# A fourth weight group taken from rounded parts, and a hand-kept list of steps made anew

## The chip, the cores and the metric

The kernel runs on one core of one Trainium2 chip. The metric is the device time of one execution in microseconds (us). An execution's time is a little longer than the span that its profile shows from the first to the last instruction; both are given below.

## What is computed

The reference has two stages. The first is a gated linear attention over 4 batches, 8 heads, 768 tokens and a head width of 48; the second is a feed-forward block on the 3072 resulting rows of width 384, with 2048 hidden columns.

```python
f = 1.0 / (1.0 + np.exp(-f_logit))
for t in range(S):
    state = f[:, :, t, :, None] * state + einsum('bhd,bhde', k[:, :, t], v[:, :, t])   # outer product
    y[:, :, t] = einsum('bhd,bhde->bhe', q[:, :, t], state)
x = y as rows (B*S, H*D)                    # 3072 x 384
h = x @ w_in                                # first product, 384 -> 2048
sp = np.maximum(h, 0.0) + np.log1p(np.exp(-np.abs(h)))
g = h * erf(sp)
out = g @ w_out                             # second product, 2048 -> 384
```

## The kernel before

**Tiling.** The tokens are cut into 24 chunks of 128 rows (numbered g), two of which make one of 12 blocks of 256 rows (blk). For a block the 2048 hidden columns are four groups of 512 (gi = 0 to 3). For every group the first product leaves a 128x1024 tile `h`; ScalarE (ACT) takes an exponential and three hyperbolic tangents, VectorE (DVE) three combining passes, and the second product multiplies the result by the rows of `w_out` that belong to the group, adding up all four groups of a block in one bank pair of PSUM. `copy_rows` and `store` then send the block's 256 output rows away. The weights come in as 64-bit numbers and are rounded at the start (the steps named `r`, on ACT and DVE).

**Plain products and products from parts.** A float32 product is done in one of two ways. *Plain*, one float32 matmul, which is two recorded instructions on TensorE (PE). *From parts*: the activation is cut into a (ACT, `part_a`), b and t (DVE, `part_b` and `part_t`), the weight into three streams, and three matmuls of the type fp32r, one recorded instruction each, are added up in PSUM. The first three blocks take the first product plain, the later nine from parts. The second product is plain in blocks 0 to 3; from block 4 on it comes from parts for the groups in `SPLIT_OUT`, which are 0, 1 and 2, and stays plain for group 3. Of a weight of the second product, one part (`form_o`) stays in SBUF in the place of the plain weight; the two others are written to `form_dram` once (`keep_form`) and fetched again by every block in pieces of 384 KB (`fetch_form`, on the POOL queue; 2 streams x 2 pieces a group).

**Buffers.** 15 slots of 128x1024 words (`slot(n, ...)`) hold the tiles e, x, h, g, the fetched pieces, kT, qA, lt and rows by turns; a slot's new owner waits until the last reader of the old one is done. PSUM is four bank pairs. Two copies of v with the running state (`sv`) and two states are used in turn; from chunk 12 on the state goes into `sv` by DMA from the SP queue (`copy_state` without an engine, L554 before), in earlier chunks by a copy on ACT or DVE.

**What sets the order.** One long list, `STEPS`, gives the program order: each token is a step (name, numbers, engine letter, and after @ the slots or bank pairs). Every engine and every DMA queue takes its own instructions strictly in the order of the list and waits for semaphores. The names used below: `d` sums of logits, `tx` transposes, `ds` state products (L571), `sc` scores (L583), `y` the attention's output rows (L634), `st` adding up the state (L547 and L548, DVE), `sp` state into `sv`, `hf`/`ht` the first product from parts (L695), `ae` exponential (L173), `ax`/`aw` the two tanh terms (L176), `at`/`au` the passes that take them in (L181), `ah` the last tanh (L726), `am` the last multiply (L730), `ka`/`kb`/`kt` the parts of the activation (L737, L741, L750), `nc`/`no` fetches (L391), `oa`/`o`/`ot` the second product (L762; `oa` with part a, `o` with b or plain, `ot` with t), `cl`/`ex`/`ln` the logits, `z` dummy matmuls (L433) that occupy PE at the start. ACT loads a table whenever it changes between `ex`/`ln` and the tanh steps.

Of the kernel before, what the change touches and what calls it, by code (L numbers as in the profile page):

```python
# [81 lines left out]
def kernel(  # L82
# [347 lines left out]
    def keep_busy(n):  # L430

        for _ in range(n):
            nc.tensor.matmul(busy[-1], lhsT=tri[:], rhs=tri[:], start=True, stop=True)  # L433
# [389 lines left out]
    def pads(_):  # L823
# [6 lines left out]
        p0 f0@0 f1 k0 zb0@0 in0 v1 r0_0 q0 cl0 r0_1 ex0 v0 r0_2 ln0 cl1 q1 r0_3 z21 d0@1 ex1 ln1  # L830
        k1 r0_4 e0 z2 d1@2 r0_5 p2 to0@1 e1 qd0 f2@0 r0_6 tq0@3 v0_0_0a p1 v0_1_1a to1@2 ta0 kd0
        aq0@1 q2 qd1 tk0 ta1 kd1 v0_0_1a ds0 ak0v@2 ds1 v0_1_0a st0 sc0 ms0 sp0a st1 tq1@3 q3
        v1_1_0a m0_1_1 v1_0_0a tk1 f3 aq1@2 st2 ak1v@3 v1_1_1a cl2 z4 sc1 v1_0_1a m0_0_0 sp1a
        m0_1_0 m0_0_1 v3 ex2 m1_1_1 r1_0 v2 m1_0_0 z7 y0_1@1 m1_0_1 ln2 k2 r1_1 y0_0 sp2a st3
        d2@3 x0a p3 m1_1_0 r2_0 y1_0@1 cl3 r1_2 k3 y1_1 e2 r2_1 w3 r1_3 p6 x1a to2@3 v2_1_1a
        v2_1_0a r2_2 p7 h0_0@1 v2_0_0a r1_4 v2_0_1a f4@2 ta2 ex3 r1_5 ln3 r2_3 sp3a r1_6 d3@0 p5
        r2_4 r3_0 h0_1 p4 qd2 r2_5 e3 r3_1 kd2 f5 tq2@0 kd3 r6_0 r2_6 tk2 aq2@0 ds2 r3_2 ds3@2
        ak2v@1 to3 qd3 c0_0a v4 r6_1 sc2 v5 r3_3 ae0_0@3 h0_2@1 m2_0_0 ax0_0@1 r3_4 m2_0_1 r3_5
        tq3@0 st4 aw0_0@4 tk3 r3_6 q5 aq3@5 m2_1_0 h0_3 k4 st5 k5 r4_0 ak3v@6 m2_1_1 sp4a r4_1
        f7@7 r5_0 ta3 sc3 r4_2 st6 y2_1@3 c0_1a y2_0 m3_0_1 sp6a m3_1_1 w4 m3_1_0 sp5a f6 m3_0_0  # L840
        y3_1@1 x2a st7 y3_0 ae0_1@0 r5_1 cl4 x3a sp7a r5_2 h1_0@1 w5 r4_3 ex4 q4 r5_3 r4_4 r7_0
        r5_4 h1_3@2 r4_5 ln4 r7_1 r5_5 r4_6 d4@3 d5@0 e4 h1_1 r5_6 p8 f8@2 kd4 r6_2 e5 qd4 r6_3
        tx4@0 c1_0a@5 r7_2 to4@3 p9 qd5 aq4@6 f9 r6_4 h1_2 ak4v@8 r6_5 r8_0 r7_3 q7 sc4 r6_6
        c1_1a@9 k6 ds4 r7_4 h0_5@0 m4_1_0 v6 r7_5 r9_0 p10 m4_0_0 r7_6 q6 h0_4 m4_0_1 p11 m4_1_1
        ta4 kd5 at0_0 k7 tx5@2 c0_2a st8 to5@1 ak5v@1 sp8a st9 ds5 aq5@8 au0_0 h0_7@3 aw0_1@10
        v7 ta5 r9_1 r8_1 r9_2 st10 sc5 sp9a r9_3 h0_6 sp10a m5_0_1 r10_0 r9_4 r11_0 m5_1_1
        m5_1_0 ax0_1@1 r10_1 y4_1@2 m5_0_0 y4_0 r10_2 c0_3a y5_0@1 w6 at0_1 y5_1 ah0_0 h1_4@3
        r10_3 ax0_2@1 am0_0 x5a x4a w7 au0_1 ae0_2@3 h1_5 r9_5 ax0_3@10 r11_1 ah0_1 r9_6 h2_2@2
        c1_2a@8 at0_2 p13 kco1@6@4 am0_1 aw0_2@1 sCo1 h1_7@3 r11_2 ae1_0@0 r10_4 r11_3 r10_5
        h2_3 r11_4 au0_2 nc4_1@11 r10_6 ah0_2 h1_6 r11_5 p14 c2_1a@1 am0_2 ax1_0@12 r11_6  # L850
        ae0_3@3 h2_0@2 at1_0 p15 c1_3a@13 at0_3 aw1_0@12 h2_4@3 r8_2 aw0_3@10 au1_0 r14_0 au0_3
        ah1_0 h2_1 r8_3 ah0_3 am1_0 r15_0 r8_4 ax1_1@10 h2_5 r15_1 r8_5 c2_0a@0 am0_3 aw1_1@12
        h2_6@2 r15_2 r13_0 r8_6 ae1_3@3 r13_1 p12 r15_3 ae1_1@14 o1_0_0@1 r13_2 at1_1 r13_3
        ax1_2@10 o0_0_1@0 r14_1 r13_4 r15_4 au1_1 r12_0 o1_0_1 r14_2 aw1_2@12 r12_1 r13_5 r12_2
        kMo1 o0_0_0 c2_2a@5 r12_3 sMo1 r13_6 ah1_1 r12_4 o0_1_0 r15_5 am1_1 kci0 kci1 r12_5
        o0_1_1 ae1_2@14 r15_6 r12_6 at1_2 o0_2_1 kci2 r14_3 ax1_3@10 au1_2 kci3 o0_2_0 at1_3
        ah1_2 aw1_3@12 r14_4 am1_2 aw2_0@10 o1_1_0 au1_3 ae2_0@14 r14_5 kci4 cl6 ah1_3 o1_1_1
        r14_6 ex6 kMi2 kMi0 o0_3_1 am1_3 ax2_0@9 cl8 kMi1 o0_3_0 kMi4 ae2_1@3 at2_0 ln6 kMi3
        o1_2_0 au2_0 ro0a@9 ax2_1@12 kDi2 ms6 d6@0 kDi0 so0 d7@3 h2_7 e6 at2_1 f11@7 ah2_0 qd6
        e7 kd6 kDi3 aw2_1@12 tx6@3 td7 am2_0 o1_3_0 q8 c2_3a@9 k8 ak6v@10 aq6@14 td6 kd7 qd7 f10  # L860
        kci6 au2_1 sc6@3 kci5 ds6 m6_0_1 tx7@2 kci7 m6_1_1 o1_2_1 kMi5 v8 aq7@10 ak7v@12 tt6
        ah2_1 m6_1_0 k9 kDi4 q9 ex8 o1_3_1 am2_1 tt7 kDi5 ax2_2@3 m6_0_0 ds7@2 st12 cl10 y6_0@0
        v9 st13 sc7 kDi1 o2_0_1@3 sp12a sp13a m7_0_1 st14 ro1a@12 m7_1_0 ae2_2@13 so1 m7_1_1
        m7_0_0 y6_1 sp14a at2_2 y7_0@1 aw2_2@8 w8 y7_1 o2_1_1 kMi6 xa6 xa7 st15 ex10 xb7 w9 xb6
        xt7 hf3_2@0 xt6 aw2_3@12 au2_2 ht3_2 hf3_0@1 ah2_2 kMi7 hf3_1 ln10 kDi6 am2_2 ht3_1
# [379 lines left out]
```

## Time and profile before

| | us |
|---|---|
| median of 3 runs (585.39 to 588.98) | 588.85 |
| the profiled execution's own time | 588.31 |
| its span, first to last instruction | 586.3 |
| PE busy | 559.7 |
| DVE busy | 465.5 |
| ACT busy | 428.9 |
| POOL busy | 106.2 |

Busy times are unions of an engine's instructions; PE's instructions are pipelined, so that its rate is read from the distance of starts and not from the durations. DMA moved 85.59 MB. All rows used further on come from this one execution.

### The profile page before, as it was taken

The page shows a single profiled execution, that of the slowest core. Times are in us where ns is not written, and L with a number is a line of the kernel's source. Part 1 is how long each engine was busy: PE and PEld are TensorE (multiplying, and loading weights), DVE is VectorE, ACT ScalarE, POOL GpSimd, SP SyncE. Part 2 cuts the span into 40 slices and gives each one's busy share as a digit, 9 for nine tenths or more (in the row PEclk, how much of TensorE's full clock was granted, in tenths as well). Part 3 has the DMA queues.
Part 4 walks back from the last instruction along what each step waited for, and adds up shares of the span by engine and source line. Part 5 has one row for each costly group of instructions (what it writes and reads, how often), then busy time and mean ns, then how long its engine had stood idle before and what let it go on. Part 6 is the DMA issues. An engine that isn't in the chain of part 4 may idle for free.

```text
span 586.3 us, 14905 instructions
## 1 busy us (share of the span) xinstructions
PE 559.7 (95%) x6189; PEld 470.5 (80%) x6189; DVE 465.5 (79%) x657; ACT 428.9 (73%) x529; POOL 106.2 (18%) x191
## 2 busy tenths in 40 slices
PE   8888999999999999999979999999998999999995
PEld 7776888855678668888859888979888979897983
DVE  6888999999995697886589889498966886686491
ACT  5768497859999875984998995678782853682781
POOL 1103021000030003033032123142233114211020
PEclk9979999999999999999989999999998999999999
DMA  8996755200540286199339669545888176565071
GB/s 212 227 262 124 188 152 183 100 27 0 115 107 1 42 232 213 55 234 224 81 86 213 177 150 220 125 128 162 218 225 188 38 182 168 166 184 155 28 200 47
DMA packets 155698, 85.59 MB, mean 146 GB/s; under 512 B 132228, under 2 KB 135300, under 8 KB 155624
## 3 DMA queue, kind: packets, MB, share of 16 engines
q1 hardware_dynamic: 139112, 42.68, 31.7%
q0 software_dynamic: 16512, 41.89, 25.5%
q8 instruction: 51, 0.84, 0.6%
q14 instruction: 23, 0.19, 0.1%
HBM read 73.41 MB, written 9.51 MB: 141 GB/s over the span
## 4 chain that ended last, share of the span: by engine, by line
PE 66%; ACT 10%; DVE 9%; DMA 7%; issue 3%; SPq 3%; POOL 0%; ACTq 0%; DVEq 0%; POOLq 0%
PE pair L762 27%; PE pair L695 21%; PE pair L676 8%; PE pair L634 3%; DVE e L181 2%; PE pair L583 2%; DMA raw_y<-in_moe_w_in_dram 2%; ACT qA L519 2%; DMA sv<-state 2%; ACT x L176 2%; PE pair L571 1%; PE pair L433 1%; DMA piece<-form_dram 1%; DVE qA L608 1%; DMA lt<-in_f_logit_dram 1%
## 5 line engine op out<-in xcount | busy, mean ns | idle before, releaser
L181 DVE SCALAR_TENSOR_TENSOR e<-x,e 128x1024 f32<-128x1024 f32 x96 | 116.6, 1219 | 36.9 <-ACT e L173 19.3
L176 ACT ACTIVATE x<-h,serf_bias 128x1024 f32<-128x1024 f32 x88 | 100.0, 1147 | 15.9 <-DVE e L181 11.0
L762 PE MATMUL pair<-plain_o,h 128*128 128x384 f32 x320 | 110.5, 493 | 0.8 <-DVE h L730 0.8
L391 POOL DMA_DIRECT2D piece<-form_dram x96 | 52.2, 545 | 282.6 <-PE pair L762 169.0
L762 PEld LDWEIGHTS pair<-plain_o,h 128*128 128x128 f32 x320 | 59.0, 191 | 37.9 <-DVE h L730 1.1
L288 POOL DMA_DIRECT2D sv<-in_v_dram x84 | 52.4, 635 | 180.2 <-PE pair L634 156.8
L762 PE MATMUL pair<-piece,g 128*128 128x384 f32 x384 | 81.6, 350 | 1.7 <-DMA piece<-form_dram 0.8
L695 PE MATMUL pair<-xT,form_x 128*128 128x256 f32 x432 | 77.0, 286 | 0.4 <-DVE xT L657 0.4
L695 PE MATMUL pair<-xT,form_i 128*128 128x256 f32 x432 | 74.1, 279 | 0.0
L762 PEld LDWEIGHTS pair<-piece,g 128*128 128x128 f32 x384 | 66.5, 191 | 5.8 <-DVE g L750 1.1
L676 PE MATMUL pair<-xT,plain_i 128*128 128x256 f32 x288 | 67.8, 394 | 1.2 <-ACT xT L137 0.8
L726 ACT ACTIVATE e<-e 128x1024 f32<-128x1024 f32 x48 | 50.5, 1055 | 21.3 <-DVE e L181 20.9
L695 PEld LDWEIGHTS pair<-xT,form_x 128*128 128x128 f32 x432 | 62.5, 188 | 4.5 <-DVE xT L657 1.4
L676 PEld LDWEIGHTS pair<-xT,plain_i 128*128 128x128 f32 x288 | 55.4, 196 | 10.4 <-ACT xT L137 1.0
L695 PE MATMUL pair<-xT,form_y 128*128 128x256 f32 x432 | 62.4, 283 | 0.0
L730 DVE TENSOR_TENSOR h<-h,e 128x1024 f32<-128x1024 f32 x44 | 53.5, 1219 | 9.5 <-ACT e L726 9.5
L695 PEld LDWEIGHTS pair<-xT,form_i 128*128 128x128 f32 x432 | 60.9, 188 | 0.0
L695 PEld LDWEIGHTS pair<-xT,form_y 128*128 128x128 f32 x432 | 56.4, 188 | 1.6 <-issue 0.3
L173 ACT ACTIVATE e<-h 128x1024 f32<-128x1024 f32 x44 | 46.1, 1051 | 12.9 <-DVE h L137 7.1
L137 ACT COPY h<-pair 128x1024 f32<-128x1024 f32 x34 | 34.2, 1009 | 21.6 <-PE pair L695 10.3
L608 DVE TENSOR_TENSOR qA<-pair,tri 64x256 f32<-64x256 f32 x96 | 40.4, 421 | 7.0 <-PE pair L571 3.3
L762 PE MATMUL pair<-form_o,g 128*128 128x384 f32 x192 | 39.8, 340 | 0.0
(104 smaller groups left out, 777.4 us busy)
## 6 DMA issues: line engine op xcount, KB each, us to landing
piece<-form_dram POOLq DMA_DIRECT2D x96, 384.0 KB, 3.9
raw_y<-in_moe_w_out_dram SPq DMA_DIRECT2D x8, 768.0 KB
kn<-in_k_dram SPq DMA_DIRECT2D x24, 192.0 KB
vt<-in_v_dram SPq DMA_DIRECT2D x24, 192.0 KB
qn<-in_q_dram SPq DMA_DIRECT2D x24, 192.0 KB
form_dram<-piece SPq DMA_DIRECT2D x12, 384.0 KB
out_dram<-rows SPq DMA_DIRECT2D x12, 384.0 KB
sv<-in_v_dram POOLq DMA_DIRECT2D x84, 48.0 KB, 3.0
```

Source lines behind the costliest of these rows:

```text
L137: (engine.copy if engine is nc.scalar else engine.tensor_copy)(out=out, in_=in_)
L173: nc.scalar.activation(out=dst[:], in_=h, func=AF.Exp)
L176: nc.scalar.activation(out=dst[:], in_=h, func=AF.Tanh, bias=serf_bias[:, i : i + 1], scale=SERF_KAB[i][0])
L181: nc.vector.scalar_tensor_tensor(out=e[:], in0=x[:], scalar=SERF_KAB[i][2], in1=e[:], op0=ALU.add, op1=ALU.mult)
L288: nc.gpsimd.dma_start(out=svs[g % NSV][half(1 - r), r, c, :, PAD : PAD + D], in_=v[b, r::2, t0 : t0 + C, :].rearrange("a t d -> t a d"),)
L391: nc.gpsimd.dma_start(out=streams[i, blk, u], in_=form_dram[i, u])
L608: nc.vector.tensor_tensor(out=to, in0=sc[half(c), r], in1=tri1[half(c)].unsqueeze(1).broadcast_to((C, HP, C)), op=ALU.mult,)
L676: nc.tensor.matmul(hts[blk, gi][:, 2 * i + j, :], lhsT=w[:, kt, j * P : (j + 1) * P], rhs=xTs[blk][:, 0, kt, :], start=(kt == 0), stop=(kt ...
L695: nc.tensor.matmul(hts[blk, gi][:, 2 * i + j, :], lhsT=w[:, kt, j * P : (j + 1) * P], rhs=x[:, kt, :], start=(blk, p) not in begun, stop=True,
L726: nc.scalar.activation(out=e[:], in_=e[:], func=AF.Tanh, scale=SERF_C)
L730: nc.vector.tensor_tensor(out=h, in0=h, in1=es.pop((blk, gi))[:], op=ALU.mult)
L762: nc.tensor.matmul(ots[blk][:, tt, 0:d_model], lhsT=lhs, rhs=rhs, start=("o", blk, tt) not in begun, stop=True, skip_group_check=True,)
```

## The change

`SPLIT_OUT` becomes (0, 1, 2, 3): from block 4 on group 3 of the second product comes from parts as well. So 8 x 1 `ka`, `kb` and `kt`, 32 fetches (`nc`, `no` with u = 6 and 7) and 64 plain products become 192 products from parts; and once, at the making of the parts, 2 more `kco`, `kMo` and `kDo` and 4 stores of 384 KB. `keep_busy` can put its dummy matmuls into a bank pair that a later step will own, and there are 43 dummy products instead of 34. The list of steps is new throughout, 1962 tokens instead of 1862, from a planning run in which the transfer times were those of the packets in a trace. The number of ACT table loads is 32 in both.

```diff
+    ahead = {}
+
     def bank_pair(n):
-        return psum.tile([P, 2, 512], FP32, name=f"pair{n}", tag=f"pair{n}")
+        return ahead.pop(n, None) or psum.tile([P, 2, 512], FP32, name=f"pair{n}", tag=f"pair{n}")
...
-    SPLIT_OUT = (0, 1, 2)
+    SPLIT_OUT = (0, 1, 2, 3)
...
-    def keep_busy(n):
-
-        for _ in range(n):
-            nc.tensor.matmul(busy[-1], lhsT=tri[:], rhs=tri[:], start=True, stop=True)
+    def keep_busy(times, n=None):
+        to = busy[-1]
+        if n is not None:
+            ahead[n] = bank_pair(n)
+            to = ahead[n][:, 0, 0:P]
+        for _ in range(times):
+            nc.tensor.matmul(to, lhsT=tri[:], rhs=tri[:], start=True, stop=True)
...
     STEPS = """
...
-        no11_5@3 kb11_2 oa11_4 oa11_5 au11_3 o11_2_0_1 kt11_2 ah11_3 o11_2_1_1 am11_3 ot11_4
-        ot11_5 o11_3_0 o11_3_1 ro11a@1 so11
...
+        nc11_6@12 oa11_5 au11_3 o11_2_1_1 nc11_7@0 o11_2_0_1 ah11_3 ot11_4 am11_3 no11_6@7
+        ot11_5 ka11_3@10@9 no11_7@1 kb11_3 oa11_6 oa11_7 kt11_3 o11_3_1_1 o11_3_0_1 ot11_6
+        ot11_7 ro11a@1 so11
     """.split()
```

Three places of the new order. First, PE at the end of the program, block 11, the last block; a row is a run of instructions, with the bank pair written and what is read: `xT` and `form_x`, `form_i`, `form_y` are the first product, `g` the parts of the activation, `piece` and `form_o` weights from parts, `plain_o` the plain weight. Before:

```order
L762 MATMUL pair_6436<-piece,g 128x384 x4
L695 MATMUL pair_6362<-xT_6269,form_y_1704 128x256 x6
L762 MATMUL pair_6436<-piece,g 128x384 x8
L816 MATMUL pair_6511<-ident,low 1x128
L762 MATMUL pair_6436<-piece,g 128x384 x4
L762 MATMUL pair_6436<-form_o_2295,g 128x384 x8
L762 MATMUL pair_6436<-piece,g 128x384 x16
L762 MATMUL pair_6436<-form_o_2354,g 128x384 x8
L762 MATMUL pair_6436<-piece,g 128x384 x8
L762 MATMUL pair_6436<-plain_o_1180,h 128x384 x8
```

The same place now:

```order
L767 MATMUL pair_6666<-piece,g 128x384 x8
L700 MATMUL pair_6558<-xT_6431,form_y_1707 128x256 x6
L767 MATMUL pair_6666<-form_o_2335,g 128x384 x8
L767 MATMUL pair_6666<-piece,g 128x384 x16
L767 MATMUL pair_6666<-form_o_2492,g 128x384 x8
L767 MATMUL pair_6666<-piece,g 128x384 x16
L767 MATMUL pair_6666<-form_o_2920,g 128x384 x8
L767 MATMUL pair_6666<-piece,g 128x384 x8
```

After the last run of the first product, 52 products from parts and 8 plain ones have become 64 from parts.

Second, ACT at the start of the third batch of sequences, where the logits of two blocks are taken (L422 and L426 before, L424 and L428 now) between the tanh terms of blocks 4 and 5; `qA` is the copy that frees a bank pair of transposes for PE. Before:

```order
L402 ACT_TABLE_LOAD
L426 ACTIVATE lt<-lt 128x768
L176 ACT_TABLE_LOAD
L176 ACTIVATE x<-h,serf_bias 128x1024
L402 ACT_TABLE_LOAD
L422 ACTIVATE lt<-lt 128x768
L176 ACT_TABLE_LOAD
L176 ACTIVATE x<-h,serf_bias 128x1024
L173 ACTIVATE e<-h 128x1024
L402 ACT_TABLE_LOAD
L426 ACTIVATE lt<-lt 128x768
L519 COPY qA<-pair_3109 64x512 x2
```

Now:

```order
L137 COPY h<-pair_2863 128x1024
L424 ACTIVATE lt<-lt 128x768
L176 ACT_TABLE_LOAD
L176 ACTIVATE x<-h,serf_bias 128x1024
L173 ACTIVATE e<-h 128x1024
L404 ACT_TABLE_LOAD
L428 ACTIVATE lt<-lt 128x768
L137 COPY h<-pair_2966 128x1024
L176 ACT_TABLE_LOAD
L176 ACTIVATE x<-h,serf_bias 128x1024
L137 COPY kT<-pair_3069 128x512
L524 COPY qA<-pair_3069 64x512 x2
```

In the twelve rows that end with the copy `qA` there were five table loads, and there are three.

Third, PE in chunks 18 and 19, the first of the last batch: `sv_86` and `sv_87` hold v and the state of the two chunks, and half of each run of 32 needs a state that a DMA brings. Before:

```order
L634 MATMUL pair_4997<-qA,sv_86 32x64 x16
L762 MATMUL pair_4848<-piece,g 128x384 x4
L634 MATMUL pair_4997<-qA,sv_86 32x64 x16
L762 MATMUL pair_4848<-piece,g 128x384 x4
L762 MATMUL pair_4848<-form_o_2295,g 128x384 x4
L634 MATMUL pair_5068<-qA,sv_87 32x64 x16
L451 MATMUL pair_5088<-lt,tri_60 64x192 x4
L762 MATMUL pair_4848<-form_o_2295,g 128x384 x4
L634 MATMUL pair_5068<-qA,sv_87 32x64 x16
```

Now:

```order
L639 MATMUL pair_5120<-qA,sv_86 32x64 x32
L767 MATMUL pair_5050<-piece,g 128x384 x8
L456 MATMUL pair_5179<-lt,tri_60 64x192 x4
L767 MATMUL pair_5050<-piece,g 128x384 x8
L456 MATMUL pair_5205<-lt,tri_60 64x192 x4
L639 MATMUL pair_5215<-qA,sv_87 32x64 x32
```

The four half runs stood apart with 4 to 8 products between them; now each chunk's two halves stand together, and between the two chunks lie 16 products of the second product and 8 sums of logits.

More of the change, by code (lines that the diff above doesn't have):

```diff
@@ L829 @@
     STEPS = """
[L830 to L865, printed above, removed]
@@ L962 @@
[L962 to L967 removed]
+        p0 f0@0 zb0@0 f1 q0 in0 v0 r0_0 v1 cl0 ex0 r0_1 k0 r0_2 ln0 cl1 k1 z27 d0@1 r0_3 ex1 ln1
```

243 lines of the change are left out of this document (143 added, 100 removed).

## The prediction

> **What bounds the kernel now.** I read the page's table of busy times first, then stretches of the span, then who waits for whom on PE.
>
> ```profile
> PE 559.7 (95%) x6189; PEld 470.5 (80%) x6189; DVE 465.5 (79%) x657; ACT 428.9 (73%) x529; POOL 106.2 (18%) x191
> ```
>
> PE leaves only 586.3 - 559.7 = 26.6 us of its span uncovered. The stretches (span, then busy time and instructions of PE, PEld, DVE, ACT, POOL, granted clock, DMA share, GB/s) say where another engine matters:
>
> ```profile
> 0.00:50.00 50.00, 43.89 (x612) 37.87 (x616) 38.73 (x82) 33.81 (x62) 4.64 (x15) 0.90 0.92 225
> 50.00:100.00 50.00, 47.27 (x573) 40.24 (x562) 49.20 (x79) 37.03 (x53) 10.32 (x17) 1.00 0.59 155
> 100.00:150.00 50.00, 50.00 (x193) 33.79 (x192) 49.64 (x62) 41.97 (x46) 0.00 (x0) 1.00 0.17 61
> 300.00:350.00 50.00, 49.58 (x572) 44.09 (x575) 44.65 (x56) 45.11 (x51) 12.38 (x22) 1.00 0.72 177
> 150.00:587.00 437.00, 418.57 (x4829) 358.59 (x4827) 327.93 (x436) 316.10 (x371) 91.20 (x159) 0.99 0.58 145
> ```
>
> The first 50 us are a start with DMA at 0.92; from 50 to 150 us PE and DVE are both nearly full; after that PE is covered for 418.6 of 437 us while DVE has 109 us to spare. The group to be changed belongs to blocks 4 to 11, all in the last stretch. So I treat the kernel as bound by PE's work plus the places where PE stands.
>
> **Term 1, the products: -7.0 us.** PE's own rate is read from the distance of starts:
>
> ```profile
> 310.90 1.56 PE L762 MATMUL pair<-form_o,g 128*128 128x384 f32 x8
> 312.30 1.55 PE L762 MATMUL pair<-piece,g 128*128 128x384 f32 x8
> 313.69 0.52 PE L695 MATMUL pair<-xT,form_x 128*128 128x256 f32 x3
> 330.60 5.43 PE L762 MATMUL pair<-plain_o,h 128*128 128x384 f32 x16
> 335.57 0.81 PE L695 MATMUL pair<-xT,form_x 128*128 128x256 f32 x3
> 121.14 13.06 PE L762 MATMUL pair<-plain_o,h_x 128*128 128x384 f32 x40
> 134.04 5.32 PE L762 MATMUL pair<-plain_o,h 128*128 128x384 f32 x16
> ```
>
> Eight products from parts take 1.40 and 1.39 us, so the 24 that replace a block's eight plain ones take 4.19 us. The eight plain ones, 16 instructions, took 335.57 - 330.60 = 4.97 us; in a long run 40 instructions took 12.90, which makes 5.16 for 16. The gain is 0.78 to 0.97 us a block, 6.2 to 7.8 us for eight. I take 7.0. It is small because three products from parts (3 x 0.174 = 0.52) cost four fifths of a plain one (0.62 to 0.645).
>
> **Term 2, added work on DVE and ACT: 0, with cover.**
>
> ```profile
> L741 DVE SCALAR_TENSOR_TENSOR g<-h,g 128x1024 fp32r<-128x1024 f32 x24 | 29.2, 1219 | 2.1 <-ACT g L737 2.1
> L750 DVE SCALAR_TENSOR_TENSOR g<-g 128x1024 fp32r<-128x1024 f32 x24 | 29.0, 1218 | 0.2
> L737 ACT ACTIVATE g<-h 128x1024 fp32r<-128x1024 f32 x24 | 25.3, 1054 | 6.4 <-DVE e L181 3.8 <-DVE h L730 2.4
> L360 DVE SCALAR_TENSOR_TENSOR piece<-plain_o,piece 128x768 fp32r<-128x768 f32 x6 | 5.7, 949 | 1.0 <-ACT piece L357 1.0
> ```
>
> DVE gets 8 `kb` and 8 `kt` at 1.22, 19.5 us, and for the two new weight pieces two `kM` and two `kD` at 0.95, 3.8 us; ACT gets 8 `ka` at 1.05, 8.4 us. DVE's share after 150 us goes from 75% to about (327.9 + 23) / 428 = 82%. The work that hides it is PE's: between 300 and 350 us DVE was busy 44.65 and ACT 45.11 of 50 us with DMA at 0.72, and PE was covered for 49.58. If that cover fails, each of the 16 passes costs up to 1.22 us, 19.5 in all.
>
> **Term 3, added fetches: +1.0 us.**
>
> ```profile
> L391 POOL DMA_DIRECT2D piece<-form_dram x96: 537/538/605, 96.9 to 569.3; - x96
> DMA to landing us min/median/max: 3.1/3.9/6.8
> PE pair L762 <- DMA piece<-form_dram: 0.8, 1, 0.8
> ```
>
> 32 more fetches of 384 KB are 12.6 MB; with four stores the kernel moves about 99.8 MB instead of 85.6, 173 GB/s, the rate that the stretch from 300 us already had. Ninety-six fetches cost PE 0.8 us of direct waiting. A third more of them at that rate is 0.3; I take 1.0; the bounds are 0 and 2.9, one piece at the maximum landing instead of the median with PE waiting for it. The queue is POOL's: behind a fetch that waits for its slot stand the other fetches and the loads of `sv`.
>
> **Term 4, the state's way by DMA: -3.0 us.**
>
> ```profile
> PE pair L634 <- DMA sv<-state: 2.0, 3, 1.5
> 439.31 0.36 DVE L548 TENSOR_TENSOR state<-state,Tall 112x192 f32<-112x192 f32 x1
> 439.41 0.56 PE L451 MATMUL pair<-lt,tri 64*64 64x192 f32 x8
> 439.89 0.96 PE L762 MATMUL pair<-form_o,g 128*128 128x384 f32 x4
> 442.34 0.30 PE L634 MATMUL pair<-qA,sv 128*32 128x64 f32 x4 [1.48 <-DMA sv<-state]
> 439.00:443.00 4.00, 2.16 (x44) 1.31 (x36) 3.97 (x7) 0.41 (x2) 1.77 (x3) 1.00 1.00 259
> 443.80:447.30 3.50, 3.50 (x12) 3.50 (x12) 3.08 (x6) 2.09 (x4) 1.83 (x3) 0.51 0.45 67
> ```
>
> In chunks 18 and 19 PE waited 2.0 us for states on their way (PE's waits between 430 and 446 us). The state was ready at 439.67 and PE went on at 442.34: 2.7 us. Right after it the granted clock was 0.51 for 3.5 us, which costs another 3.5 x 0.49 = 1.7. In the new order the 16 products of the second product and two chunks' sums of logits (439.89 - 439.41 = 0.48 each) stand between the two chunks, 16 x 0.174 + 0.96 = 3.7 us, longer than 2.7. So up to 3.7 goes; I take 3.0, bounds 0 (a later state) and 3.7.
>
> The Trainium skill, "TensorE: Matmul & The Clock Gate", section "Why this matters for your kernels", asks for no idle gap of TensorE over about 3 us, since one idle window puts it back to half clock. The trace is stricter here: the longest gap was 1.48 us in a stretch with 2.16 of 4.0 us busy, and the clock fell. By that rule the place would be worth 2.0 at most, and the sum 1 us smaller. I go by the row.
>
> **Term 5, the table loads of batch three: -2.5 us.**
>
> ```profile
> PE pair L571 <- ACT qA L519: 3.3, 1, 3.3
> 289.74 1.28 ACT L176 ACT_TABLE_LOAD   x1
> 295.19 1.15 ACT L519 COPY qA<-pair 64x512 f32<-64x512 f32 x2
> 297.00:300.50 3.50, 3.50 (x106) 2.91 (x98) 2.41 (x7) 3.43 (x4) 1.12 (x2) 0.51 0.13 27
> ```
>
> PE's longest wait anywhere, 3.3 us, is for the copy `qA` behind ACT's alternating tables, again followed by 3.5 us at a clock of 0.51: 3.3 + 1.7 = 5.0 us. In the new order two of the five loads ahead of the copy are gone, 2 x 1.28 = 2.6 us, but a copy of h and one of kT have come in. I take half, 2.5; bounds 0 and 5.0.
>
> **Term 6, the end: +1.0 us.**
>
> ```profile
> 562.45 1.55 PE L762 MATMUL pair<-piece,g 128*128 128x384 f32 x8
> 572.62 1.23 DVE L730 TENSOR_TENSOR h<-h,e 128x1024 f32<-128x1024 f32 x1
> 574.19 5.32 PE L762 MATMUL pair<-plain_o,h 128*128 128x384 f32 x16
> 579.54 0.80 ACT L137 COPY rows<-pair 128x768 f32<-128x768 f32 x1 [6.96 <-PE pair L762]
> ```
>
> From the first start after the block's first product (562.45) to PE's end (579.5) lie 17.05 us, in which PE has 52 x 0.174 + 5.2 = 14.3 us of work: 2.8 idle. Now it has 64 x 0.174 = 11.1. The last group's chain goes by these rows of the page, and `ka` and the copy as above:
>
> ```profile
> L181 DVE SCALAR_TENSOR_TENSOR e<-x,e 128x1024 f32<-128x1024 f32 x96 | 116.6, 1219 | 36.9 <-ACT e L173 19.3
> L176 ACT ACTIVATE x<-h,serf_bias 128x1024 f32<-128x1024 f32 x88 | 100.0, 1147 | 15.9 <-DVE e L181 11.0
> L726 ACT ACTIVATE e<-e 128x1024 f32<-128x1024 f32 x48 | 50.5, 1055 | 21.3 <-DVE e L181 20.9
> L173 ACT ACTIVATE e<-h 128x1024 f32<-128x1024 f32 x44 | 46.1, 1051 | 12.9 <-DVE h L137 7.1
> ```
>
> It is: copy 1.0, `ka` of group 2 1.05, `ae` 1.05, `ax` and `aw` 2.3, `au` 1.22 (DVE may still hold `kb`, `kt` and `at`: 0.4 more), `ah` 1.05, `am` 1.23, `ka` 1.05, then three runs of eight, 4.2, and 0.8 of passing on: about 15.3, 4.1 idle. So the end gives back 1.3; I take 1.0, bounds -1 and +3.
>
> **Term 7, the start: +0.5 us.** The nine extra dummies are 18 instructions of this row, 11.0 / 68 x 18 = 2.9 us, in a stretch of which PE lacked 6.1:
>
> ```profile
> L433 PE MATMUL pair<-tri 128*128 128x128 f32 x68 | 11.0, 330 | 1.6 <-POOL tri L1007 1.6
> ```
>
> I take 0.5, bounds 0 and 2.9. The order of the start is new as well; DVE's full 50 to 150 us keep the same instructions, so I expect no change there, within 3 us both ways (half of the 6.1 us that PE lacked in the first 50).
>
> **Sum.** -7.0 + 0 + 1.0 - 3.0 - 2.5 + 1.0 + 0.5 = -10.0: a span of 576.3 us. The profiled execution was 2.0 us longer than its span (588.31) and lies 0.5 below the median; so about 578 us, 1.8% less than 588.85.
>
> **The rivals.**
>
> *Given back to new waits (chance 0.25): 585 us.* Every engine's order is new; the two places may be paid at others. For it: PE takes `o` only after `kb` and `ot` after `kt`, DVE is fuller, and the slots now hold a, b, t and four pieces more for each block. Against it: 300 to 350 us. Term 1 alone then stays, with terms 3, 6 and 7: 586.3 - 4.5 + 1.2 (one pass exposed) + 2.0 = 585.
>
> *The products are not what ends last (0.07): 588 us.* Then the chain of ACT and DVE, not PE, sets the pace of a block, and what PE saves it waits. Against it speaks PE's 418.6 of 437 us.
>
> *Slower, by late pieces (0.10): 601 us.* The place is each new group's last pieces: in the list, `no11_6` stands ahead of `ot11_6` by `ot11_5`, `oa11_6`, `oa11_7` and two `o`, 20 products or 3.5 us, and landing took 3.9 in the median. With landing at the maximum, 6.8, two pieces in each of eight blocks would cost 16 x 1.45 = 23 us, if half of the 2.9 us of difference is hidden by work beside it; 586.3 - 10 + 23 + 2 = 601. It makes the kernel slower by over 1% from about 1 us a piece, a landing near 5.9. Against it: 177 GB/s at 300 us without waits. The Trainium skill, "SBUF — State Buffer", section "Who interferes with whom" and its box on DMAs from GpSimd, says that such a queue can be locked out while DVE holds the shared port, which would speak for this rival since DVE gets 23 us more. The trace does not show it: the 96 issues took 537 to 605 ns beside a DVE busy for 79% of the span.
>
> *Better (0.10): 572 us.* Terms 4 and 5 in full and the start 3 us shorter: 578 - 0.7 - 2.5 - 3.
>
> **How the numbers follow.** The likeliest, 574 to 583 us, has 0.48. This kernel's runs differ by up to 0.6%, so 1% (583 to 594.7) is about what can be told from no change. Faster by over 1%: 0.48 + 0.10 = 0.58; within 1%: 0.25 + 0.07 = 0.32; slower: 0.10. The range 570 to 592 leaves out the slower rival and the tail of the better one.
>
> **What would show it.** The group of `L762` on `plain_o,h` falls by 128 recorded instructions, the one on pieces rises by as many; PE's busy time falls by about 6; no wait of PE for `sv<-state` over 1 us and at most one stretch of half clock after 50 us; PE's wait for `qA` under 2 us; landing near 4 us. Wrong I am if PE's waits for `g` (L741, L750) or `piece` add up to more than 5 us, or if the first plain product of `w_in` starts over 3 us later than before.

## The result and the profile after

| | before | after |
|---|---|---|
| median, 12 executions each side by side | 587.30 us (585.39 to 592.90) | 584.22 us (579.65 to 588.44) |
| ratio after/before | | 0.9923, 95% interval 0.9894 to 0.9953 |
| span of the profiled execution | 586.3 | 582.4 |

The change makes the kernel 0.8% faster, 3.1 us by the medians and 4.5 by the ratio; the forecast was 578, 1.8%. The direction is right, the size less than half. The ratios leave out executions more than 1.5% above the fastest of their kernel (here one, 588.44), the medians include them.

The page's busy line:

```profile
PE 553.5 (95%) x6271; PEld 477.7 (82%) x6271; DVE 487.5 (84%) x678; ACT 438.6 (75%) x538; POOL 125.9 (22%) x223
```

Two stretches of the span (busy time of PE, PEld, DVE, ACT, POOL, granted clock, DMA share, GB/s):

```profile
0.00:50.00 50.00, 41.71 (x578) 36.01 (x578) 36.24 (x78) 30.48 (x59) 6.58 (x16) 0.93 0.83 210
150.00:583.00 433.00, 413.52 (x4901) 366.46 (x4899) 352.69 (x461) 330.14 (x386) 109.25 (x191) 1.00 0.72 180
```

PE's busy time fell by 6.2 us, the "about 6" of the prediction; but at half clock (a granted clock of 0.5) the same work stays busy for longer (three 128x256 products 0.84 us instead of 0.52 in e9, 391 to 395 us), and the execution before had more of it (below), so this fall does not measure the products. DVE's busy time rose by 22, ACT's by 9.7, near what was worked out. But the stretch after 150 us was to lose about 10 us, and the whole span lost 3.9.

**Where the time went, by three marks on PE.** The rows give first and last start: first plain product of `w_in` (`plain_i`), first product from parts (`form_x`), last product of all. Of before:

```profile
L676 PE MATMUL pair<-xT,plain_i x288: 379/379/793, 27.1 to 150.3; 128*128 128x256 f32 x144
L695 PE MATMUL pair<-xT,form_x x432: 276/279/576, 171.0 to 558.5; 128*128 128x256 f32 x144
L762 PE MATMUL pair<-plain_o,h x320: 485/486/992, 113.4 to 579.0; 128*128 128x384 f32 x160
```

Of after:

```profile
L681 PE MATMUL pair<-xT,plain_i x288: 379/379/634, 31.4 to 118.6; 128*128 128x256 f32 x144
L700 PE MATMUL pair<-xT,form_x x432: 276/279/577, 174.0 to 555.7; 128*128 128x256 f32 x144
L767 PE MATMUL pair<-piece,g x512: 331/336/630, 249.7 to 575.3; 128*128 128x384 f32 x171
```

The first plain product is 4.3 us late and the first product from parts 3.0. From there to the last product it takes 408.0 us before and 401.3 after: 6.7 us less. 3.0 - 6.7 = -3.7, the gain in the profile. So the start took back almost half of what came behind it.

Half clock has to be taken out before these marks are compared. Behind the mark at 171 us the execution before has two stretches of 3.4 us at half clock, the two that the prediction shows at 297 and 444 us, which cost about 3.4 us together; the changed kernel has none there until 580 us. So 6.7 is 3.4 of half clock and 3.3 of everything else. The waits that the profile lists for PE behind that mark add up to 10.0 us before and 10.6 after: the waits of terms 4 and 5, 5.3 us, do not appear as a net gain.

**What PE waits for now** (total, times, longest):

```profile
PE pair L639 <- issue: 2.7, 1, 2.7
PE pair L588 <- DVE kT L137: 2.6, 3, 1.2
PE pair L639 <- DMA sv<-state: 2.3, 2, 1.5
PE pair L767 <- ACT g L742: 2.0, 3, 1.5
PE pair L700 <- DVE xT L662: 1.7, 1, 1.7
PE pair L456 <- DVE xT L662: 1.0, 1, 1.0
PE pair L767 <- DMA piece<-form_dram: 0.7, 1, 0.7
```

The 3.3 us for `qA` are gone, the wait for `piece` is as small as before (0.7 after 0.8). The total for states is 2.3 us again, 1.5 of it now in chunk 21 at 487 us, and new are 2.7 us of "issue" in the start and 2.7 for `xT`.

**The start.** PE and ACT, in order of time; `lt` is the logits' tile, L428 its last pass, L448 the sums that wait for it:

```profile
1.65 8.84 PE L438 MATMUL pair<-tri 128*128 128x128 f32 x54 [1.65 <-POOL tri L1021]
7.70 0.53 ACT L428 ACTIVATE lt<-lt 128x384 f32<-128x384 f32 x1
10.32 0.81 PE L448 MATMUL pair<-lt,tri 128*128 128x384 f32 x2
11.16 0.49 ACT L465 ACTIVATE dp<-pair 128x384 f32<-128x384 f32 x1 [1.61 <-PE pair L448]
28.12 1.07 PE L639 MATMUL pair<-qA,sv 128*32 128x64 f32 x28 [2.68 <-issue]
```

The logits are ready at 8.23 us, but PE is still in its 54 dummy instructions; the sums come 2.1 us later, and ACT waits 1.61 for them. Before, the sums stood at 8.95, so they are 1.4 us later now. Then, in the second half of chunk 1's output, PE stands 2.68 us waiting for nothing that the profile shows. Half clock stands in both starts. Before, in two stretches:

```profile
13.80:17.20 3.40, 3.40 (x100) 3.07 (x99) 1.58 (x5) 1.40 (x5) 0.00 (x0) 0.50 1.08 354
37.70:44.50 6.80, 6.48 (x45) 5.18 (x46) 6.61 (x14) 5.11 (x5) 0.00 (x0) 0.50 0.85 227
```

After:

```profile
27.50:34.30 6.80, 6.18 (x41) 4.87 (x41) 3.87 (x6) 3.40 (x8) 1.92 (x4) 0.50 0.93 267
```

That is 10.2 us at half clock before and 6.8 after, about 1.7 us less lost. By this estimate the new start is behind by 3.0 + 1.7 = 4.7 us at the same clock, and 1.4 for the later sums with 2.7 for the stall make 4.1 of it.

**Chunk 17**, where the new wait for `xT` is (`d18` is L456, `hf8_1` the first L700):

```profile
388.90 0.56 PE L456 MATMUL pair<-lt,tri 64*64 64x192 f32 x8 [1.01 <-DVE xT L662]
391.83 1.21 DVE L735 TENSOR_TENSOR h<-h,e 128x1024 f32<-128x1024 f32 x1
392.96 0.54 DVE L662 SCALAR_TENSOR_TENSOR xT<-pair,xT 128x384 fp32r<-128x384 f32 x1
393.56 0.62 PE L700 MATMUL pair<-xT,form_x 128*128 128x256 f32 x3 [1.66 <-DVE xT L662]
```

`d18` waits for the first of DVE's passes on `xT` (388.29), which stands behind a memset; `hf8_1` waits for the second (392.96), which stands behind a pass of the feed-forward block (L735). Each PE run needs the bank pair that the pass before it frees.

### The profile page after: what moved, and what is told of

The parts are those of the page before. It is cut to its first block, busy times and chain, and to the rows that moved or that the text cites. A ratio compares the mean times of both kernels' runs of the same rounds, so it can differ in the third digit from the quotient of the medians.

```text
span 582.4 us, 15189 instructions
## 1 busy us (share of the span) xinstructions
PE 553.5 (95%) x6271; PEld 477.7 (82%) x6271; DVE 487.5 (84%) x678; ACT 438.6 (75%) x538; POOL 125.9 (22%) x223
## 5 line engine op out<-in xcount | busy, mean ns | idle before, releaser
L393 POOL DMA_DIRECT2D piece<-form_dram x128 | 70.3, 550 | 257.0 <-PE pair L767 157.7
L767 PE MATMUL pair<-piece,g 128*128 128x384 f32 x512 | 106.6, 343 | 3.7 <-ACT g L742 2.0
L290 POOL DMA_DIRECT2D sv<-in_v_dram x84 | 54.0, 653 | 186.8 <-PE pair L639 161.2
L767 PEld LDWEIGHTS pair<-piece,g 128*128 128x128 f32 x512 | 86.6, 188 | 9.1 <-ACT g L742 3.2
L700 PE MATMUL pair<-xT,form_x 128*128 128x256 f32 x432 | 76.1, 284 | 1.7 <-DVE xT L662 1.7
L700 PE MATMUL pair<-xT,form_i 128*128 128x256 f32 x432 | 74.1, 279 | 0.0
L681 PE MATMUL pair<-xT,plain_i 128*128 128x256 f32 x288 | 66.6, 389 | 1.2 <-DVE plain_i L353 0.6
L700 PEld LDWEIGHTS pair<-xT,form_x 128*128 128x128 f32 x432 | 62.7, 188 | 4.1 <-DVE xT L662 2.1
L767 PE MATMUL pair<-plain_o,h 128*128 128x384 f32 x192 | 65.9, 492 | 0.0
L735 DVE TENSOR_TENSOR h<-h,e 128x1024 f32<-128x1024 f32 x44 | 53.7, 1221 | 11.4 <-ACT e L731 11.2
L700 PE MATMUL pair<-xT,form_y 128*128 128x256 f32 x432 | 61.7, 281 | 0.4 <-DVE xT L668 0.4
L700 PEld LDWEIGHTS pair<-xT,form_i 128*128 128x128 f32 x432 | 60.9, 188 | 0.0
L700 PEld LDWEIGHTS pair<-xT,form_y 128*128 128x128 f32 x432 | 56.2, 188 | 0.9 <-DVE xT L668 0.6
L767 PEld LDWEIGHTS pair<-plain_o,h 128*128 128x128 f32 x192 | 35.3, 190 | 23.0 <-issue 0.8
L767 PE MATMUL pair<-form_o,g 128*128 128x384 f32 x256 | 52.5, 340 | 0.0
L742 ACT ACTIVATE g<-h 128x1024 fp32r<-128x1024 f32 x32 | 33.5, 1055 | 21.3 <-DVE h L735 14.7
```

What stands on the lines that cost most here:

```text
L290: nc.gpsimd.dma_start(out=svs[g % NSV][half(1 - r), r, c, :, PAD : PAD + D], in_=v[b, r::2, t0 : t0 + C, :].rearrange("a t d -> t a d"),)
L393: nc.gpsimd.dma_start(out=streams[i, blk, u], in_=form_dram[i, u])
L681: nc.tensor.matmul(hts[blk, gi][:, 2 * i + j, :], lhsT=w[:, kt, j * P : (j + 1) * P], rhs=xTs[blk][:, 0, kt, :], start=(kt == 0), stop=(kt ...
L700: nc.tensor.matmul(hts[blk, gi][:, 2 * i + j, :], lhsT=w[:, kt, j * P : (j + 1) * P], rhs=x[:, kt, :], start=(blk, p) not in begun, stop=True,
L735: nc.vector.tensor_tensor(out=h, in0=h, in1=es.pop((blk, gi))[:], op=ALU.mult)
L742: nc.scalar.activation(out=gps_[blk, gi][0][:], in_=hs[blk, gi], func=AF.Copy, scale=KAPPA / PART)
```

## The experiments

Each ratio is to the kernel before on the same chip. The medians of one kernel differ by about 1 us between comparisons, so that less than 2 us is not told apart.

**The new list alone.** All steps of group 3's parts are taken out of the new list:

```diff
-    SPLIT_OUT = (0, 1, 2, 3)
+    SPLIT_OUT = (0, 1, 2)
     STEPS: without ka/kb/kt4_3..11_3, nc/no/oa/ot4_6..11_7, kco/kMo/kDo/sCo/sMo6, 7; o4_3_0_1 -> o4_3_0 ...
```

> The new list with the fourth group plain again (its ka, kb, kt, fetches and parts taken out, everything else in the new order). Measured so far: before 587.3 us, after 584.2. Theory A, my sum: the list alone brings terms 4 to 7 (-4.0), the products the rest, so this gives about 583 and the fourth group was worth nothing more. Theory B, the list is no better than the old one in the waits of PE and the two repaired places are paid elsewhere, while the products are worth their 6 to 8 us: about 590, 6 slower than after. Theory C, the list is better but the fourth group's own loads (DVE, fetches) eat most of what its products save: 584 to 586, near after. PE's uncovered time between 150 and 550 us: B as after, C clearly less than after.

Measured: 590.56 us, ratio 1.0086 (1.0049 to 1.0124): slower than before. Its marks:

```profile
L700 PE MATMUL pair<-xT,form_x x432: 276/279/579, 171.7 to 560.3; 128*128 128x256 f32 x144
L767 PE MATMUL pair<-plain_o,h x320: 483/486/590, 127.8 to 579.7; 128*128 128x384 f32 x160
```

and its place in chunk 17, in order of time, the clock there, and a wait in batch three that neither kernel had at this length:

```profile
390.39 0.56 PE L456 MATMUL pair<-lt,tri 64*64 64x192 f32 x8 [1.92 <-DVE xT L662]
395.06 0.58 PE L700 MATMUL pair<-xT,form_x 128*128 128x256 f32 x1 [3.05 <-DVE xT L662]
393.40:400.20 6.80, 5.14 (x24) 5.15 (x25) 6.53 (x9) 6.44 (x8) 2.30 (x4) 0.50 1.10 264
L767 PE MATMUL pair<-piece,g 128*128 128x384 f32 x384 | 79.1, 342 | 3.4 <-ACT kd L465 2.2
```

From the first product from parts to the last product it takes 408.0 us, as with the old list: the middle of the new list is worth nothing by itself, as theory B had it. The account is the same too: PE's listed waits behind the mark add up to 9.8 us (10.0 before), and 6.8 us at half clock in chunk 17 stand for the two stretches of 3.4. With group 3's products gone from between, the wait in chunk 17 is 3.05 us instead of 1.66. Group 3 from parts is worth 590.56 - 584.22 = 6.3 us by the medians, 9.6 by the ratios with some 3 us of uncertainty; about 3 us of it go with the clock, which was 0.986 in the mean of e1's executions and 0.991 in the changed kernel's.

**The two old places, mended on the old list.**

```diff
-    ex14 ... ln14 ... ex16 ... ln16            (e4: batch three's logits in one table visit)
+    ex14 ln14 ex16 ln16
-    y19_1 xt18 ot8_2 kb8_2 k23 xa19 w21 ot8_3   (e5)
+    xt18 ot8_2 ot8_3 y19_1 kb8_2 k23 xa19 w21
```

> The old kernel with the four exponential and logarithm steps of batch three (ex14, ln14, ex16, ln16) put one behind the other: six table loads fewer there, 7.7 us off ACT. Term 5 as I priced it: PE's wait of 3.3 us for qA and the 3.4 us of half clock go, 5 us faster than before, about 582. If PE is elastic, so that work not done at one place is waited for at the next: the wait goes, the time falls by less than 1.5 us, 586 to 587.

> The kernel before with one place mended: the second half of chunk 19's attention output (y19_1), which waited 1.85 us for a state on its way by DMA at 442 us and was followed by half clock for 3.5 us, is put behind the eight products ot8_2 and ot8_3 (8 x 0.174 = 1.4 us). Theory A, every wait of TensorE costs its own length: 1.4 us of the wait go, and the half clock (1.7 us) too if the gap is what brings it; 587.4 - 1.4 to - 3.1 = 584.3 to 586.0. Theory B, what is saved at one place is lost at the next: 587.4, and the waits of TensorE after 447 us are longer by as much.

Measured: e4 584.85, ratio 0.9931 (0.9895 to 0.9967), and e5 585.43, 0.9966 (0.9938 to 0.9995). On the old list the tables are worth 2.5 to 4 us and the state's place about 2: near terms 5 and 4, with e4 short of the 5 us expected, between its two theories.

**Mending the new list's places.** e6 moves chunk 17's handover, e8 lets ACT copy the states, e7 takes the nine dummies back.

```diff
-    ms18 aw7_1 v19 xb16 m17_0_1 d18 ae7_2 au7_1 y17_0 ... y17_1 no7_1 xt16 w19 xa17 am7_1 ... xb17   (e6)
+    m17_0_1 aw7_1 v19 xb16 y17_0 ae7_2 y17_1 d18 xa17 ... xb17 au7_1 at7_2 ms18 ... xt16 w19 am7_1
-    z27 ... z4 ... z2@0                         (e7)
+    z21 ... z3
-    sp24 sp25 ...                               (e8)
+    sp24a sp25a ...
```

> The changed kernel with one place of its new list mended, chunk 17 (387 to 394 us): there TensorE waits 1.17 and 1.86 us, 3.0 in all, for parts of xT that VectorE makes behind a memset and behind passes of the feed-forward block. xb16 goes ahead of the memset, xb17 ahead of au7_1, at7_2 and am7_1, both halves of y17 ahead of the logits' sums d18. Theory A, every wait costs its own length: 584.2 - 2.5 = 581.7, the first product with the new xT (393.56) about 2.5 us earlier, last product of TensorE as much earlier. Theory B, the pace after 350 us is set by VectorE and ScalarE and a gap closed opens elsewhere: 584.2 within 0.8, and the waits behind 394 us grow by about 2.5.

> The changed kernel with the 9 extra dummy products taken back (34 instead of 43: 27 become 21, 4 become 3, 2 that stood in the next step's bank pair go). Theory A, the dummies are paid in full, since TensorE is what ends last: 18 instructions at about 0.11 us are 2.0 us, so 582.2. Theory B, they fill time in which TensorE waits for the start's loads anyway: 584.2, as the prediction's term of 0.5 has it. Rival: without them the granted clock falls in the start, 585 to 587.

> The changed kernel with all copies of the state into sv done by ScalarE instead of a DMA (44 copies of about 0.25 us, ScalarE +11 us, 44 transfers of 36 KB in small pieces fewer). Theory A, every wait costs its own length: TensorE's waits for sv<-state (2.3 us in two, and the stall of 1.66 at 485 us) go, 584.2 - 2 = 582.2. Theory B, the pace is set by VectorE and ScalarE: ScalarE's 11 us come on top in part, 584 to 588. Rival C, the small packets of these transfers hold up the pieces: more than 2 us faster, 580 to 581, with a shorter landing of the pieces than 4.2 us in the median.

e6: 587.49, ratio 0.9993 (0.9961 to 1.0025), no gain, and slower than either theory had it. Two rows show new waits:

```profile
391.53 1.45 PE L639 MATMUL pair<-qA,sv 128*32 128x64 f32 x32 [1.12 <-DMA sv<-state]
400.71 1.57 PE L700 MATMUL pair<-xT,form_y 128*128 128x256 f32 x11 [2.47 <-DVE xT L668]
```

`y17_1`, moved forward, now meets the state that is still on its way, and the third part of `xT` (`xt17`, L668) is late instead of the second. The waits change place; that e6 is some 3 us slower than the changed kernel is more than that, and stays open.

e7: 582.77, ratio 0.9938 (0.9906 to 0.9970). With 34 dummies the sums of the logits come as soon as ACT is done:

```profile
7.54 0.52 ACT L428 ACTIVATE lt<-lt 128x384 f32<-128x384 f32 x1
8.11 0.91 PE L448 MATMUL pair<-lt,tri 128*128 128x384 f32 x2
```

```profile
L681 PE MATMUL pair<-xT,plain_i x288: 379/379/631, 28.5 to 116.0; 128*128 128x256 f32 x144
```

By the second view the first plain product is 2.9 us earlier (28.5 for 31.4). The first product from parts is 2.9 us earlier too (171.1 for 174.0). But this execution took 586.42 us and lost the lead again: from there to the last product it needs 406.5 us, the changed kernel 401.3. By the medians the gain is 1.4 us against the changed kernel, by the ratio to before none, so the test does not decide between its theories.

e8: 584.78, ratio 0.9951 (0.9916 to 0.9987). No wait for `sv<-state` is left on PE, and the time is the same, theory B: PE's waits for `kT` are 3.9 us instead of 2.6, those of `piece` products for `kd` 1.7 instead of 0.5.

**Relief for the transfers and for DVE.** Half the bytes of each fetch, in the changed kernel (e2), in before (e10) and in the new list alone (e14); no second pass `au` in blocks 4 to 11, in the same three (e3, e11, e15); and both in the changed kernel (e12). These leave work out, as the expectations say.

```diff
-            nc.gpsimd.dma_start(out=streams[i, blk, u], in_=form_dram[i, u])
+            nc.gpsimd.dma_start(out=streams[i, blk, u][:, 0:d_model], in_=form_dram[i, u][:, 0:d_model])
-                    add_rows(blk, tt, token_half(gps_[blk, gi][2 * f][:], 2 * i + j, tt), m[:, j, :])
+                    add_rows(blk, tt, token_half(gps_[blk, gi][2 * f][:], 2 * i + j, tt), m[:, 0, :])
     STEPS: without au4_0 .. au11_3                       (e3, e11, e15; e12 has both)
```

> The new kernel, but each fetch brings half of its piece (192 KB instead of 384) and both products of a piece use that half; the output is another one. Takes 25 MB of 99.8 MB away, all instructions stay. If the new waits come from the fuller DMA (share 0.72 after 150 us instead of 0.58): 4 us or more faster than after, about 580, with landings under 3.5 us. If they come from the order of the engines: within 1 us of after, 583 to 585.

> The new kernel without the DVE pass that takes in the second tanh term (L181, i = 1) in blocks 4 to 11; the output is another one. Takes 32 x 1.22 = 39 us off DVE and a step off each group's chain. If a fuller DVE (81% after 150 us) makes the waits: at least 4 us faster than after, 580 or less, and PE's waits for DVE shrink. If PE's waits are made by the order and by short handovers in the attention steps: no more than 2 us faster.

> The kernel before with fetches of half the bytes (each fetch brings 384 of 768 columns, and the products read that half twice, so the output is not the reference's). The same edit made the changed kernel about 4 us faster (580.4). Theory A, the traffic that the change adds (32 fetches, 12.6 MB) is what costs: before gains 1.5 us or less, 586. Theory B, the fetches cost as much in the old list, so the change adds little with its own: before gains 3 us or more (three quarters of 4), 584 or less.

> The kernel before without the second combining pass (au) of blocks 4 to 11, 39 us of VectorE's work, whose result is left out of the output. The same edit made the changed kernel about 5 us faster (579.3). Theory A, VectorE's added 22 us in the changed kernel are what its waits come from: before, with more room, gains 2 us or less, 585.5 or more. Theory B, VectorE holds up TensorE as much before: a gain of 4 to 5, 583.

> The changed kernel with both reliefs, half the bytes of every fetch and no second pass in blocks 4 to 11 (its output leaves those out). If VectorE's load and the transfers cost separate waits, the gains add up: 584.2 - 4 - 5 = 575. If both act on the same waits, 578 to 579. If TensorE's waits in the middle come from the order itself and not from what the others have to do, the waits between 150 and 550 us stay above 20 us (27.5 in the changed kernel, 23.3 with half the bytes).

> The new list with the fourth group left plain (e1, 590.6) and half the bytes of every fetch (so the output is not the reference's). Theory A, the new list itself has its fetches ahead of their use: a gain of 4 as in the changed kernel, 586.5. Theory B, the gain goes with the number of fetches that the list places, not with the list: about 10 as in the kernel before, 580.5.

> The new list with the fourth group left plain (e1, 590.6), without the second combining pass of blocks 4 to 11 (39 us of VectorE's work, left out of the output). Theory A, it is the new list that hangs on VectorE: a gain of 5 as in the changed kernel, 585.5. Theory B, it is the 22 us that the fourth group's parts add on VectorE: a gain of 1 or less as in the kernel before, 590.

| | half the bytes | no second pass | both |
|---|---|---|---|
| before | 576.83, 0.9828 (0.9780 to 0.9875) | 589.56, 0.9995 (0.9956 to 1.0035) | |
| new list alone (590.56, 1.0086) | 590.43, 1.0056 (1.0025 to 1.0086) | 589.81, 1.0025 (0.9995 to 1.0054) | |
| changed kernel (584.22, 0.9923) | 580.37, 0.9859 (0.9804 to 0.9914) | 579.25, 0.9851 (0.9799 to 0.9903) | 576.13, 0.9796 (0.9758 to 0.9835) |

The old list gains about 10 us from lighter fetches (theory B of e10, and more) and nothing from DVE's relief (theory A of e11). Its profile with half the bytes, marks and the longest of the old waits:

```profile
L695 PE MATMUL pair<-xT,form_x x432: 276/279/576, 167.3 to 546.8; 128*128 128x256 f32 x144
L762 PE MATMUL pair<-plain_o,h x320: 483/486/590, 109.7 to 567.4; 128*128 128x384 f32 x160
```

```profile
PE pair L571 <- ACT qA L519: 1.0, 1, 1.0
```

From first product from parts to last: 400.1 us instead of 408.0, and the wait for `qA` is 1.0 instead of 3.3; all listed waits there are 6.4 us instead of 10.0. The other 3.7 us lie ahead of it, where only a few fetches run. They go with the clock: this execution had no half clock before 571 us, where the one before had lost about 5.1 us in the start and 3.4 behind it. Over all executions the granted clock was 0.993 in e10 and 0.986 before, worth about 4 of the 10 us; whether shorter waits bring that was not tried. The new list alone gains nothing that can be told from lighter fetches, which neither theory of e14 had:

```profile
L700 PE MATMUL pair<-xT,form_x x432: 276/280/584, 171.9 to 561.3; 128*128 128x256 f32 x144
L767 PE MATMUL pair<-plain_o,h x320: 482/486/592, 127.9 to 580.7; 128*128 128x384 f32 x160
```

408.8 us with half the bytes, 408.0 with all. So the new list, made from the packets' transfer times, no longer hangs on transfers, and yet is no shorter: with all its fetches it takes the time that the old one takes with all of its own. With group 3's parts on top, each relief is worth 4 to 5 us and both together 8.1, nearly their sum; with half the bytes the landing falls from 4.2 to 2.8 us. That the new list alone gains less, 0 to 1 us by the medians, speaks for the work that the fourth group adds. By the ratios it gains 2 and 4 us, so for the transfers the contrast is likely and for DVE it is not shown.

**The start.** e9 (and e17, the same kernel once more) puts the old list's first 97 steps before the rest of the new list; e13 does the reverse on the old list; e16 adds a second try at chunk 17 to e9, e18 the states by ACT.

```diff
     STEPS of e9: the old list up to y1_0 (z21 z2 z4 z7, slots 0 and 1 of lt and qA exchanged),
+    r1_2 y1_1 r2_1
     then the new list from r2_2 on
-    xb16 m17_0_1 d18 ae7_2 au7_1 y17_0 ... y17_1 ... xt16 w19 xa17 am7_1 ... xb17 ... xt17      (e16)
+    m17_0_1 ... xb16 y17_0 ae7_2 y17_1 ms18 xt16 d18 xa17 ... xb17 xt17 au7_1 at7_2 ... am7_1
```

> The changed kernel with the first 97 steps of the old list (up to the attention output of chunk 1, the loads 34 dummy products instead of 43) in front of the new list's rest. In the new start the first sums of the logits run at 10.32 us, behind 54 dummy instructions that follow each other without a wait, while they run at 8.1 to 8.9 us with 42; and TensorE stands 2.4 to 4.1 us at 25 us, which the old start does not have. Theory A, TensorE's start is paid in full: 584.2 - 2.0 (dummies) - 2.4 (the stall) = 579 to 580. Theory B, the start waits for loads and VectorE anyway: 584.2 within 1, the waits up to 60 us longer.

> The kernel before with the changed kernel's start (its first 102 steps, 43 dummies) ahead of the old list's rest. Theory A, the new start costs what the old start gave the changed kernel: 587.5 + 5 = 592 to 593, with first sums of logits at 10.3 us and a stall of 2.4 to 4 us near 25 us. Theory B, the new start fits only badly to what follows in the new list: 587.5 within 1.5.

> The changed kernel with the old start (578.9) and with chunk 17's handover mended: xb16, xt16, xb17 and xt17 ahead of au7_1, at7_2 and am7_1, both halves of y17 ahead of d18. TensorE's waits of 1.2 and 2.1 us at 384 and 388 us can go. Theory A, the order can take them away: 578.9 - 2.5 = 576.4. Theory B, VectorE is full there (384 to 402 us without a gap) and the wait turns up at the next pass it owes: 578.9 within 1, with a new wait of 1 us or more between 388 and 405 us.

> The changed kernel with the old start once more, unchanged. If the gain is the start's own (2.0 us of dummies and the stall at 25 us of 2.4 us or more): 579 to 580.5, 1.3% or more below the kernel before. If the 5 us were half clock that one program load met and another doesn't: 582 to 584, with half clock before 60 us in the profile.

> The changed kernel with the old start and all copies of the state into sv by ScalarE. Theory A, waits for states also bring half clock (3.41 us at half clock are 1.7 us), and without them both go: 1 to 3 us faster than the run beside it with the old start alone. Theory B, ScalarE's 11 us more cost what the waits gave: the same within 1 us.

e9: 578.90 us, ratio 0.9849 (0.9806 to 0.9891); e17: 580.91, 0.9877 (0.9836 to 0.9918). Marks of e9, then of e17:

```profile
L681 PE MATMUL pair<-xT,plain_i x288: 379/379/483, 26.0 to 111.9; 128*128 128x256 f32 x144
L700 PE MATMUL pair<-xT,form_x x432: 276/279/576, 166.8 to 550.4; 128*128 128x256 f32 x144
L767 PE MATMUL pair<-piece,g x512: 331/336/630, 242.6 to 570.1; 128*128 128x384 f32 x171
```

```profile
L700 PE MATMUL pair<-xT,form_x x432: 276/279/577, 168.0 to 551.6; 128*128 128x256 f32 x144
L767 PE MATMUL pair<-piece,g x512: 331/336/660, 243.8 to 572.8; 128*128 128x384 f32 x171
```

and e17's stretch at half clock:

```profile
14.20:21.00 6.80, 6.80 (x115) 6.10 (x113) 3.78 (x10) 3.22 (x9) 0.00 (x0) 0.50 0.92 237
```

The first product from parts comes 7.2 and 6.0 us earlier than in the changed kernel. e17 lost 6.8 x 0.5 = 3.4 us to half clock in its start, as much as the changed kernel did from 27.5 us on, and is still 6.0 us ahead of it at this mark; e9 lost none, so that 3.4 of its 7.2 are the clock's. In the end the two are 5.3 and 3.3 us faster than the changed kernel by the medians, 4.4 and 2.7 by the ratios: a gain of the start's own, though e17 is a little short of what was expected of it.

e13: 590.40, 1.0051 (1.0010 to 1.0092), about 2 to 3 us slower than before, between its theories. Its executions had the better clock, 0.991 against 0.987 beside it; at the same clock the loss is about 5 us, near theory A. So the new start costs on the old list too. e16: 584.19, 0.9937 (0.9905 to 0.9969), no gain again: the wait for `xT` is gone and PE waits in the next place,

```profile
397.25 1.67 PE L767 MATMUL pair<-piece,g 128*128 128x384 f32 x8 [2.25 <-ACT g L742]
```

for the part of a group whose passes had been put back; that it is 3 to 5 us slower than e9 and e17 is more than this wait. PE's waits for states also rose, to 4.7 us from 1.5 and 1.8; what each is worth stays open. e18: 578.91, ratio 0.9830 (0.9784 to 0.9877), 2.0 us less than e17 beside it, though the intervals overlap. The time is theory A's, its reason is not: the profile still has half clock, at 341.5 to 348.3 and 392.7 to 396.1 us. It beats both kernels, by 5.3 us (after) and 8.6 us (before, on its chip).

## Why the prediction was right or wrong, point by point

- **Term 1 (products, -7.0): right in kind, too large.** The 6.7 us from mark to mark contain 3.4 of half clock, and e1's profile has as much. I had taken the rate from undisturbed runs of eight, 0.174 us. Over all products behind the mark, without listed waits and half clock, one from parts took 0.187 (`piece`) and 0.184 (`form_o`) in the changed kernel, and one instruction of a plain one 0.314 before: 24 x 0.186 = 4.46 for 16 x 0.314 = 5.02, about 4.5 us for eight blocks by this estimate.
- **Term 7 (the start, +0.5): the first step that failed.** Measured +3.0 at the first product from parts, about 4.7 at the same clock; with the old start in front of the same list the time is 3.3 to 5.3 us less. The dummies were priced by what PE lacked in the first 50 us (6.1), as if they fell into gaps. They stand ahead of the first sums of the logits, on which ACT, DVE and PE all depend: these come 2.1 us after the logits are ready and 1.4 later than before. How much of the time the dummies alone cost is not shown (e7). The 2.68 us of "issue" behind it no row of before showed. My own sign, the first plain product over 3 us later, came true (4.3).
- **Terms 4 and 5 (-5.5): the second step that failed.** Both waits are gone from their places and so is the half clock behind them; on the old list the repairs gave 2.5 to 4 us (e4) and about 2 (e5). But PE's listed waits behind the start add up to 10.6 us after 10.0, and the new list alone has 9.8, half clock for half clock, and needs the same 408.0 us. I had read two places of one list and taken the rest of the other list as free of waits; what I had from the order was that products stand between, not when DVE would be done. My sign "no wait for `sv<-state` over 1 us" failed as well (1.5). What happened is the rival "given back to new waits", 585 with a chance of 0.25, as far as the waits go; that its number fits so well is luck, since it too had 7.0 for the products and 0.5 for the start.
- **Term 3 (fetches, +1.0) and term 2 (DVE and ACT, 0): too small.** The relief runs gave 4 and 5 us in the changed kernel against 0 to 1 by the medians (2 and 4 by the ratios) in the same list without group 3. They take away more than was added (half of all bytes; 39 us of passes against 23), so 4 and 5 are not the price itself, and for DVE the price stays open.
- **Term 6 (the end, +1.0): right.** From the first start after the block's first product (560.49) to PE's end (575.64) lie 15.1 us, where I had 15.3; 11.1 of them are work, so 4.0 are idle after 2.8, +1.2. The waits for a piece and for the last group's first part add up to 2.2:

```profile
560.49 1.56 PE L767 MATMUL pair<-form_o,g 128*128 128x384 f32 x8
568.76 0.97 PE L767 MATMUL pair<-piece,g 128*128 128x384 f32 x4 [0.72 <-DMA piece<-form_dram]
571.19 1.67 PE L767 MATMUL pair<-piece,g 128*128 128x384 f32 x8 [1.46 <-ACT g L742]
574.08 1.56 PE L767 MATMUL pair<-piece,g 128*128 128x384 f32 x8
575.68 0.80 ACT L137 COPY rows<-pair 128x768 f32<-128x768 f32 x1 [4.54 <-PE pair L767]
```

- **Late pieces (the slower rival): did not happen.** Landing is near 4 us as forecast, PE waits 0.7 for pieces, and the issues are not held up with DVE at 84%:

```profile
L393 POOL DMA_DIRECT2D piece<-form_dram x128: 540/540/865, 101.5 to 570.0; - x128
DMA to landing us min/median/max: 3.1/4.2/7.1
```

  The lock-out that the Trainium skill, "SBUF — State Buffer", section "Who interferes with whom", tells of for such queues, while DVE is in a two-port mode, shows in neither the median issue (540 ns) nor the landing (4.2 us).
- **The sum.** 588.85 - 10.0 is 578.9, not 578; this changes nothing above.

## What to carry to other kernels

Price work at the start by the first instruction that everything else waits for, not by the idle time of its stretch: nine more dummies moved the marks behind them by 2.9 us, and the whole new start cost 3 to 5 us. A wait that goes away is worth its length only where the next engine due is early; look in the new order at what each engine owes there, and compare the sum of all waits (10.0, 9.8 and 10.6 us here), not the places that were read in the old list. To see what a list hangs on, relieve one resource at a time on both lists: here the old list gained about 10 us from lighter transfers and the new one none, which the waits' own totals did not tell. And read the granted clock before two profiles are compared: 17.0 us at half clock ahead of PE's last product in one and 6.8 in the other are about 5 us, more than the 3.9 by which their spans differ.
